# Sharing out the splitting of weights by direct and mirrored pairs, and an MLP that begins four steps later

## The chip, the cores and the metric

One core of a Trainium2 chip. The metric is device time in microseconds of the slowest (here the only) core.

## The reference

Four sequences of 3008 tokens. First an attention without softmax, then an MLP over all 12032 tokens:

```python
scores = (1.0 / S) * z @ z.T            # z: 4 x 3008 x 64
attn   = np.maximum(scores, 0.0) ** 2   # symmetric
x      = u * (attn @ v)                 # u, v: 4 x 3008 x 256
h      = x @ w_in                       # 256 -> 2048, w_in is float64
g      = h * np.clip(h + 3.0, 0.0, 6.0) / 6.0
y      = g @ w_out                      # 2048 -> 256, w_out is float64
```

## The kernel before

**Splitting.** Each operand of a matmul is split into a high and a low part of a reduced-precision type, and a product is made of three matmuls (low times high, high times low, high times high). So every `h`, `y` and `o` tile costs three passes on TensorE (PE), and VectorE (DVE) has to make every low part (`al`, `gl`, `xl`, `vl`, `w_in_l`, `w_out_l`).

**Steps.** The attention of a sequence is cut into 6 *chunks* of 512 columns (`c`), and a chunk into 12 *pairs* of 2 x 128 rows (`p`). There are 24 chunks and 288 steps, numbered through as `g`; step 12 begins chunk 1, step 24 chunk 2, step 36 chunk 3. In step g, `attend` multiplies pair g by `v` (12 matmuls into the two PSUM banks `o0` and `o1`), while `scores` works ahead on a later pair: two ahead as long as `g < FIRST`, one ahead from then on (`lead`). After the last pair of a chunk, `times_u` (L388, two DVE instructions) reads both banks, and only then can the first matmul of the next chunk write into them.

**Two kinds of pair.** A *direct* pair (`p // 2 >= c`) is computed: 4 matmuls `s`, then on ScalarE (ACT) three instructions `rt` (Relu, L320), `ah` (Square, rounded, L329) and `r` or `r2` (Square, L330), then on DVE one `al` (L340). A *mirrored* pair (`p // 2 < c`) is the transposed copy of one already computed in this sequence: no `s` matmuls, but a turn on DVE (L271), a cast on ACT (L285) and `al` on DVE (L287). Chunk 0 has no mirrored pair, chunk 1 the pairs 0 and 1, chunk 2 the pairs 0 to 3, chunk 3 the pairs 0 to 5.

**Weights.** `w_in` and `w_out` come in as float64, in 16 pieces, and each has to be split once: `split64` takes 6 DVE operations a piece (L101, L106, L110, L114, L119, L123), `finish64` two more (L131, L133), 8 in all, and one ACT cast (L117) that reads what L114 has written and that L131 waits for. The generator `weight_ops` hands them out one DVE operation at a time; `weight_work(n)` issues the next n. A piece is finished only after the next one has been split. The ACT cast is not issued where it arises but put in a list, which `flush_copies` empties: in `scores`, behind the pair's ACT instructions, or at the start of `finish64`, whichever comes first in the program. Pieces are fetched by the SP queue two pieces ahead.

**MLP.** 16 *units* a chunk of tokens: 8 times `up` (12 matmuls `h`, ACT L418, DVE L419, ACT L77, DVE `gl` L78) and 8 times `down` (12 matmuls `y`). Units are issued at the end of a step, so many that they are spread evenly over the steps from `FIRST` on; the last 20 units come after the last step. The line that says how many are to be done after step g:

```python
target = max(0, g + 1 - FIRST) * ((len(chunks) - 1) * NU - 4) // total   # total = 288 - FIRST, NU = 16
```

The order of instructions on each engine is the order of the program (`manual_schedule`); nothing is reordered later. In one step it is: `scores` of a later pair, the turn of the pair after it, `weight_work`, `attend` and `times_u`, MLP units.

Of the kernel before, what the change touches and what calls it, by code (L numbers as in the profile page):

```python
# [19 lines left out]
NPAIR = NJ // 2  # L20
# [1 line left out]
NF = DFF // P  # L22
NFP = NF // 2

FIRST = 28

TINY = 1.125 * 2.0 ** -15

# [2 lines left out]
def relu2_attention_then_hswish_mlp(  # L31
# [153 lines left out]
    def split_v(b, p):  # L185
        vh, raw = vt[b, p], raws.pop(("v", p))
        vl = vpool.tile([P, 2, D], F32R, tag="vl", name="vl")
        split(vh, vl, raw, rounded=b == 0)
        vt[b, p] = (vh, vl)

    def fetch_z(b, k):
        if b == 0:
            raw = xpool.tile([P, CH], F32, tag=("xh0", "xh1", "xl0", "xl1")[k % 4], name="zraw")
        else:
            raw = stg.tile([P, CH], F32, tag="stg", name="zraw")
        zx = zpool.tile([P, CH], F32R, tag="zx", name="zx")
        zy = zpool.tile([P, CH], F32R, tag="zy", name="zy")
        zt[b, k] = (zx, zy)
        raws["z", k] = raw
        cols = slice(k * CH, (k + 1) * CH)  # L200
        nc.sync.dma_start(out=raw, in_=zz[b, :, cols])
        if b == 0 and k > 1:
            nc.gpsimd.dma_start(out=zx[0:64], in_=zz[b, 0:64, cols])
            nc.gpsimd.dma_start(out=zy[64:128], in_=zz[b, 64:128, cols])

    def split_z(b, k):
        zx, zy = zt[b, k]
        raw = raws.pop(("z", k))
        split(zx[0:64], zy[0:64], raw[0:64], b == 0 and k > 1)
        split(zy[64:128], zx[64:128], raw[64:128], b == 0 and k > 1)  # L210
# [13 lines left out]
    def fetch_mirrored():  # L224

        while to_fetch and len(mirrored) < 2:
            b, c, p = to_fetch[0]
            if (b, p // 2, c) not in whole:
                return
            fetch_pair(*to_fetch.pop(0))  # L230

    def fetch_pair(b, c, p):


        src = kept[b, p // 2, c]
        nk = width(c) // 32
        t = lpool.tile([P, 16, 64], F32, tag="l", name="l")
        for q in range(4):
            c0 = q * P + (p % 2) * 64
            nc.sync.dma_start(  # L240
                out=t[32 * q:32 * q + 32, :nk, :],
                in_=src[:, c0:c0 + 64].rearrange("(k e) f -> e k f", e=32),
            )
        mirrored[b, c, p] = t
# [19 lines left out]
    def turn(b, c, p):  # L264

        if p // 2 >= c:
            return
        n = width(c)
        t = mirrored.pop((b, c, p))
        rn = rpool.tile([P, 2, CH], F32, tag="r", name="rm")[:, :, :n]  # L270
        nc.vector.transpose(  # L271
            out=rn.rearrange("p r (k e) -> p r k e", e=32),
            in_=t[:, :n // 32].rearrange("p k (r e) -> p r k e", r=2),
        )
        turned[b, c, p] = rn
        fetch_mirrored()

    def from_mirror(b, c, p):
        n = width(c)
        rn = turned.pop((b, c, p))  # L280
        ah = apool.tile([P, 2, CH], F32R, tag="ah", name="ah")
        al = apool.tile([P, 2, CH], F32R, tag="al", name="al")
        if urgent:
            flush()
        nc.scalar.copy(out=ah[:, :, :n], in_=rn)  # L285
        flush_copies()
        nc.vector.tensor_tensor(  # L287
            out=al[:, :, :n], in0=rn, in1=f(ah[:, :, :n]), op=ALU.subtract
        )
        at[b, c, p] = (ah, al)  # L290
        flush()
# [62 lines left out]
    def width(c):  # L354
        return CH if c < NCH - 1 else S - CH * (NCH - 1)
# [20 lines left out]
    def load_u(b, c):  # L376
        n = width(c)
        t0 = b * S + c * CH
        t = upool.tile([P, 2, CH], F32, tag="u", name="u")
        nc.sync.dma_start(  # L380
            out=t[:, :, :n], in_=ut[:, t0:t0 + n].rearrange("(k p) t -> p k t", p=P)
        )
        raw_x[b, c] = t
# [8 lines left out]
    def split_x(b, c):  # L392
        n = width(c)
        raw = raw_x.pop((b, c))
        for d in range(2):
            xh = xpool.tile([P, CH], F32R, tag=f"xh{d}", name=f"xh{d}")
            xl = xpool.tile([P, CH], F32R, tag=f"xl{d}", name=f"xl{d}")
            split(xh[:, :n], xl[:, :n], raw[:, d, :n])
            xt[d] = (xh, xl)
# [54 lines left out]
    pairs = [(b, c, p) for b, c in chunks for p in range(NPAIR)]  # L454
# [62 lines left out]
    def weight_work(n):  # L517
        for _ in range(n):
            next(w_ops, None)
# [17 lines left out]
    def maybe_split():  # L537

        if to_split and to_split[0] < avs[0]:
            i = to_split.pop(0)  # L540
            split_x(*chunks[i])
            if i + 2 < len(chunks):
                load_u(*chunks[i + 2])

    def attend(b, c, p):
        for d in range(2):
            av(b, c, p, d)
            if p == NPAIR - 1:
                times_u(b, c, d)
# [3 lines left out]
    def turn_next():  # L553

        while g_turned[0] < min(g_done + 1, len(pairs)):
            turn(*pairs[g_turned[0]])
            g_turned[0] += 1

    with tc.manual_schedule():
        nc.vector.memset(three, 3.0)  # L560
        fetch_z(0, 0)
        fetch_v(0, 0)
        split_z(0, 0)
        fetch_z(0, 1)
        fetch_v(0, 1)
        weight_work(1)
        split_v(0, 0)
        split_z(0, 1)
        scores(0, 0, 0)
        fetch_z(0, 2)  # L570
        fetch_v(0, 2)
        scores(0, 0, 1)
        fetch_v(0, 3)
        g_done = 2
        to_fetch += [(b, c, p) for b, c, p in pairs if p // 2 < c]
        g_turned = [2]
        for i, (b, c) in enumerate(chunks):
            ahead = b + 1 if c == NCH - 1 and b + 1 < B else None
            for p in range(NPAIR):
                g = i * NPAIR + p  # L580
                lead = 2 if g < FIRST else 1
                if i == 0:
                    if p + 1 < NPAIR:
                        split_v(0, p + 1)
                    if p % 2 == 0 and p // 2 + 2 < NCH:
                        split_z(0, p // 2 + 2)
                early = lead == 2 and p == NPAIR - 1
                if early:
                    attend(b, c, p)
                while g_done < min(g + lead + 1, len(pairs)):  # L590
                    scores(*pairs[g_done], square_on_act=i < 3)
                    g_done += 1
                if p > 3:
                    fetch_mirrored()
                if p < NPAIR - 1 or early:
                    turn_next()
                if i == 0:
                    if p + 4 < NPAIR:
                        fetch_v(0, p + 4)
                    if p % 2 == 0 and p // 2 + 3 < NCH:  # L600
                        fetch_z(0, p // 2 + 3)
                    if p == 6:
                        load_u(*chunks[0])
                        load_u(*chunks[1])
                maybe_split()
                if g >= FIRST:
                    weight_work(5)
                elif p < NPAIR - 2:
                    weight_work(4 if i else 2)
                if ahead and p < NPAIR - 1:  # L610
                    if p:
                        split_v(ahead, p - 1)
                    if p < NPAIR - 2:
                        fetch_v(ahead, p)
                    if p % 2 == 1:
                        fetch_z(ahead, p // 2)
                    elif p:
                        split_z(ahead, p // 2 - 1)
                elif b and c == 0 and p < 4:
                    if p in (1, 2):  # L620
                        split_v(b, NPAIR - 3 + p)
                    if p < 2:
                        fetch_v(b, NPAIR - 2 + p)
                    if p == 2:
                        fetch_z(b, NCH - 1)
                    if p == 3:
                        split_z(b, NCH - 1)
                if not early:
                    attend(b, c, p)
                    turn_next()  # L630
                if p == NPAIR - 1:
                    avs[0] += 1
                total = len(pairs) - FIRST
                target = max(0, g + 1 - FIRST) * ((len(chunks) - 1) * NU - 4) // total
                mlp_units(target - units_done[0])
        mlp_units(1)
        maybe_split()
        mlp_units(len(chunks) * NU - units_done[0])
# [35 lines left out]
```

## Time and profile before

| | |
|---|---|
| time, median of 3 runs (lowest, highest) | 1997.01 us (1996.62, 1998.65) |
| the profiled execution's own time | 1998.23 us |
| its span | 1996.4 us |
| mean granted TensorE clock | 0.994 |
| PE busy | 1959.4 us (98%) |
| DVE busy | 1280.7 us (64%) |
| ACT busy | 987.5 us (49%) |

The span runs from the first to the last instruction of the profiled execution. Busy time of an engine is the sum of its instructions; a group's idle time is what its engine stood still just before it, and the releaser named is what ended that. The chain of waits is followed back from the last instruction, at each step to what released it. Times in the timeline are microseconds from the start of the span.

### The profile page before, as it was taken

The page shows a single profiled execution, that of the slowest core. Times are in us where ns is not written, and L with a number is a line of the kernel's source. Part 1 is how long each engine was busy: PE and PEld are TensorE (multiplying, and loading weights), DVE is VectorE, ACT ScalarE, POOL GpSimd, SP SyncE. Part 2 cuts the span into 40 slices and gives each one's busy share as a digit, 9 for nine tenths or more (in the row PEclk, how much of TensorE's full clock was granted, in tenths as well). Part 3 has the DMA queues.
Part 4 walks back from the last instruction along what each step waited for, and adds up shares of the span by engine and source line. Part 5 has one row for each costly group of instructions (what it writes and reads, how often), then busy time and mean ns, then how long its engine had stood idle before and what let it go on. Part 6 is the DMA issues. An engine that isn't in the chain of part 4 may idle for free.

```text
span 1996.4 us, 22062 instructions
## 1 busy us (share of the span) xinstructions
PE 1959.4 (98%) x8688; PEld 1637.0 (82%) x8688; DVE 1280.7 (64%) x1277; ACT 987.5 (49%) x1057; POOL 14.2 (1%) x26
## 2 busy tenths in 40 slices
PE   7899999999999999999999999999999999999999
PEld 5677788788888888888888888888888888888888
DVE  5798765676556566577565665657756565666654
ACT  6665444455444444456544454444554544444343
POOL 2000000000000000000000000000000000000000
PEclk9899999999999999999999999999999999999999
DMA  9663233424323233253333232324342323332300
GB/s 266 201 160 103 64 82 72 115 71 116 82 64 81 72 74 95 50 128 89 95 82 90 55 93 53 101 62 109 90 116 61 86 59 92 74 82 60 94 10 20
DMA packets 403271, 178.14 MB, mean 89 GB/s; under 512 B 250080, under 2 KB 385248, under 8 KB 403168
## 3 DMA queue, kind: packets, MB, share of 16 engines
q1 hardware_dynamic: 399232, 172.55, 34.3%
q0 software_dynamic: 3936, 4.20, 0.9%
q8 instruction: 68, 1.11, 0.2%
q14 instruction: 35, 0.29, 0.1%
HBM read 104.07 MB, written 72.61 MB: 89 GB/s over the span
## 4 chain that ended last, share of the span: by engine, by line
PE 90%; DVE 4%; DMA 2%; ACT 2%; issue 1%; SPq 1%; DVEq 0%; ACTq 0%
PE o L73 34%; PE h L73 24%; PE y L73 24%; PE s L73 7%; DMA zraw<-in_zz_dram 1%; DVE rm L271 1%; DMA vraw<-in_v_dram 1%; DVE rt L419 1%; DVE al L287 1%; ACT rt L418 0%; ACT gh L77 0%; ACT rt L320 0%; SPq L240 0%; DVE gl L78 0%; DMA d<-r 0%
## 5 line engine op out<-in xcount | busy, mean ns | idle before, releaser
L419 DVE SCALAR_TENSOR_TENSOR rt<-rt,h 128x1024 f32<-128x1024 f32 (+1 forms) x192 | 230.0, 1198 | 420.6 <-ACT rt L418 420.4
L418 ACT ACTIVATE rt<-h,three 128x1024 f32<-128x1024 f32 (+1 forms) x192 | 211.0, 1099 | 550.2 <-PE h L73 544.4
L73 PE MATMUL o<-ah,vl 128*128 128x512 f32 (+1 forms) x1152 | 448.1, 389 | 13.3 <-DVE u L388 6.2
L73 PE MATMUL o<-ah,vh 128*128 128x512 f32 (+1 forms) x1152 | 446.8, 388 | 0.0
L73 PE MATMUL o<-al,vh 128*128 128x512 f32 (+1 forms) x1104 | 429.2, 389 | 3.5 <-DVE al L287 3.5
L73 PE MATMUL y<-gh,w_out_l 128*128 128x512 f32 (+1 forms) x768 | 296.3, 386 | 1.7 <-DVE w_out_l L133 1.7
L73 PE MATMUL y<-gl,w_out_h 128*128 128x512 f32 (+1 forms) x768 | 296.3, 386 | 1.1 <-DVE gl L78 1.1
L73 PE MATMUL y<-gh,w_out_h 128*128 128x512 f32 (+1 forms) x768 | 296.0, 385 | 0.0
L73 PE MATMUL h<-xh,w_in_l 128*128 128x512 f32 (+1 forms) x768 | 295.9, 385 | 0.0
L73 PE MATMUL h<-xl,w_in_h 128*128 128x512 f32 (+1 forms) x768 | 295.9, 385 | 0.0
L73 PE MATMUL h<-xh,w_in_h 128*128 128x512 f32 (+1 forms) x768 | 295.8, 385 | 0.0
L78 DVE TENSOR_TENSOR gl<-rt,gh 128x1024 fp32r<-128x1024 f32 (+1 forms) x192 | 230.7, 1202 | 80.5 <-ACT gh L77 77.9
L73 PEld LDWEIGHTS o<-ah,vl 128*128 128x128 f32 x1152 | 218.2, 189 | 60.6 <-issue 11.9
L77 ACT CAST gh<-rt 128x1024 fp32r<-128x1024 f32 (+1 forms) x192 | 197.2, 1027 | 122.8 <-DVE rt L419 122.8
L73 PEld LDWEIGHTS o<-ah,vh 128*128 128x128 f32 x1152 | 218.3, 189 | 40.9
L73 PEld LDWEIGHTS o<-al,vh 128*128 128x128 f32 x1104 | 209.0, 189 | 45.8 <-DVE al L287 5.7
L320 ACT ACTIVATE rt<-s 128x1024 f32<-128x1024 f32 x168 | 171.3, 1020 | 129.9 <-PE s L73 125.1
L332 DVE TENSOR_TENSOR r<-rt 128x1024 f32<-128x1024 f32 (+1 forms) x140 | 170.0, 1214 | 95.7 <-ACT rt L320 95.6
L340 DVE TENSOR_TENSOR al<-r,ah 128x1024 fp32r<-128x1024 f32 x140 | 171.0, 1221 | 22.3 <-ACT r L330 8.6
L73 PEld LDWEIGHTS y<-gh,w_out_l 128*128 128x128 f32 x768 | 144.2, 188 | 29.8 <-DVE w_out_l L133 1.3
L73 PEld LDWEIGHTS y<-gl,w_out_h 128*128 128x128 f32 x768 | 144.2, 188 | 28.9 <-DVE gl L78 2.1
L73 PEld LDWEIGHTS y<-gh,w_out_h 128*128 128x128 f32 x768 | 144.2, 188 | 27.1
(51 smaller groups left out, 1807.0 us busy)
## 6 DMA issues: line engine op xcount, KB each, us to landing
d<-r SPq DMA_DIRECT2D x220, 256.0 KB, 2.9
l<-d SPq DMA_DIRECT2D x320, 128.0 KB, 3.3
l<-d SPq DMA_DIRECT2D x160, 112.0 KB, 2.9
vraw<-in_v_dram SPq DMA_DIRECT2D x44, 256.0 KB, 3.3
u<-in_ut_dram SPq DMA_DIRECT2D x20, 512.0 KB, 4.2
out_dram<-y SPq DMA_DIRECT2D x40, 256.0 KB, 3.1
zraw<-in_zz_dram SPq DMA_DIRECT2D x24, 256.0 KB, 3.6
wraw<-in_w_in_dram SPq DMA_DIRECT2D x8, 512.0 KB, 4.5
```

The costliest lines, as they stand in the source:

```text
L73: nc.tensor.matmul(out, lhsT=lhsT, rhs=rhs, start=start, stop=stop)
L77: nc.scalar.copy(out=hi, in_=raw)
L78: nc.vector.tensor_tensor(out=lo, in0=raw, in1=f(hi), op=ALU.subtract)
L271: nc.vector.transpose(out=rn.rearrange("p r (k e) -> p r k e", e=32), in_=t[:, :n // 32].rearrange("p k (r e) -> p r k e", r=2),)
L287: nc.vector.tensor_tensor(out=al[:, :, :n], in0=rn, in1=f(ah[:, :, :n]), op=ALU.subtract)
L320: nc.scalar.activation(out=rn, in_=s[:, :, :n], func=AF.Relu, scale=1.0 / S)
L332: nc.vector.tensor_tensor(out=r2_of, in0=r_of, in1=r_of, op=ALU.mult)
L340: nc.vector.tensor_tensor(out=l_of, in0=r2_of, in1=h_of, op=ALU.subtract)
L418: nc.scalar.activation(out=rn, in_=h, func=AF.Relu, bias=three)
L419: nc.vector.scalar_tensor_tensor(out=rn, in0=rn, scalar=6.0, in1=h, op0=ALU.min, op1=ALU.mult)
```

## The change

Three things are changed. `FIRST` goes from 28 to 32, so that MLP units begin with step 32 (and `lead` becomes 1 there). In the steps of chunks 1 and 2 before `FIRST`, the number of weight operations no longer is 4 in the pairs 0 to 9 and 0 in the pairs 10 and 11, but depends on the kind of the pair scored last (two ahead of the step): 5 where it is direct, 1 where it is mirrored. From `FIRST` on it is 5 where the pair scored last is direct and 4 where it is mirrored, in place of 5 always. The steps of chunk 0 stay as they are.

```diff
-FIRST = 28
+FIRST = 32
...
+    def is_mirrored(b, c, p):
+        return p // 2 < c
...
                 maybe_split()
+                direct = not is_mirrored(*pairs[g_done - 1])
                 if g >= FIRST:
-                    weight_work(5)
-                elif p < NPAIR - 2:
-                    weight_work(4 if i else 2)
+                    weight_work(5 if direct else 4)
+                elif i == 0:
+                    weight_work(2 if p < NPAIR - 2 else 0)
+                else:
+                    weight_work(5 if direct else 1)
```

Weight operations by step: before, 40 in the steps 12 to 21, none in 22 and 23, 16 in 24 to 27, 5 a step from 28 on. Now 50 in the steps 12 to 21, 4 in 22 to 25, 30 in 26 to 31, 15 in 32 to 34, 4 in 35 and in 36, and the rest in 37. In front of the step 36 the MLP has done 11 units before, 5 now.

How this moves instructions, at three places. The numbers behind the names tell tiles apart; line numbers of the changed kernel are 3 higher from L276 on.

**First place: ACT, between the pairs 15 and 16** (chunk 1). `rt_...`, `ah_...`, `r2_...` are the three instructions of a direct pair, `w_in_h<-t0_646` is the cast of a weight piece. Before:

```order
L320 ACTIVATE rt_696<-s_691 128x1024
L329 ACTIVATE ah_697<-rt_696 128x1024
L330 ACTIVATE r2_700<-rt_696 128x8x4x32
L117 CAST w_in_h_91<-t0_646 128x2x256
L320 ACTIVATE rt_732<-s_727 128x1024
```

Now:

```order
L117 CAST w_in_h_91<-t0_646 128x2x256
L323 ACTIVATE rt_701<-s_696 128x1024
L332 ACTIVATE ah_702<-rt_701 128x1024
L333 ACTIVATE r2_705<-rt_701 128x8x4x32
L323 ACTIVATE rt_735<-s_730 128x1024
```

The cast has moved from behind the three instructions of pair 16 to ahead of them, since the step now issues L114 and the next piece's L131 together. The same happens at pair 19 and at pair 32; at the pairs 17, 20 and 22 the cast stays behind.

**Second place: DVE, from the last pair of chunk 1 to its `times_u`** (L388, L391 now). Before:

```order
L344 TENSOR_TENSOR al_935<-r2_937,ah_934 128x512
L347 TENSOR_TENSOR ah_934<-r2_937,ah_934 64x512
L271 STREAM_TRANSPOSE rm_944<-l_560 128x1024
L110 TENSOR_SCALAR wraw_842<-wraw_842 128x512
L114 SCALAR_TENSOR_TENSOR t0_913<-wraw_842,t0_913 128x512
L119 TENSOR_SCALAR wraw_842<-t0_913 128x512
L123 SCALAR_TENSOR_TENSOR w_in_l_92<-wraw_842 128x2x256
L287 TENSOR_TENSOR al_968<-rm_944,ah_967 128x1024
L271 STREAM_TRANSPOSE rm_972<-l_587 128x1024
L388 TENSOR_TENSOR u_449<-u_449,o0_649 128x512
L388 TENSOR_TENSOR u_449<-u_449,o1_656 128x512
```

Now:

```order
L350 TENSOR_TENSOR ah_947<-r2_950,ah_947 64x512
L271 STREAM_TRANSPOSE rm_957<-l_560 128x1024
L114 SCALAR_TENSOR_TENSOR t0_925<-wraw_854,t0_925 128x512
L119 TENSOR_SCALAR wraw_854<-t0_925 128x512
L123 SCALAR_TENSOR_TENSOR w_out_l_94<-wraw_854 128x512
L131 TENSOR_TENSOR t0_858<-t0_858,w_in_h_91 128x512
L133 TENSOR_TENSOR w_in_l_92<-t0_858,w_in_l_92 128x2x256
L290 TENSOR_TENSOR al_985<-rm_957,ah_984 128x1024
L271 STREAM_TRANSPOSE rm_988<-l_587 128x1024
L101 TENSOR_SCALAR t0_995<-wraw_921 128x512
L391 TENSOR_TENSOR u_449<-u_449,o0_650 128x512
L391 TENSOR_TENSOR u_449<-u_449,o1_657 128x512
```

Between the pair's `al` and `times_u` stand six weight operations now, four before; from the start of chunk 1 to `times_u` it is 51, and it was 40.

**Third place: DVE, up to the `times_u` of chunk 2.** `al_1517` and `al_1449` are of pair 36, L419 and L78 (L422 and L78 now) belong to the MLP. Before:

```order
L133 TENSOR_TENSOR w_out_l_94<-t0_1312,w_out_l_94 128x512
L101 TENSOR_SCALAR t0_1490<-wraw_1358 128x512
L287 TENSOR_TENSOR al_1517<-rm_1477,ah_1516 128x1024
L106 SCALAR_TENSOR_TENSOR t0_1490<-wraw_1358,t0_1490 128x512
L110 TENSOR_SCALAR wraw_1358<-wraw_1358 128x512
L114 SCALAR_TENSOR_TENSOR t0_1490<-wraw_1358,t0_1490 128x512
L119 TENSOR_SCALAR wraw_1358<-t0_1490 128x512
L123 SCALAR_TENSOR_TENSOR w_out_l_94<-wraw_1358 128x512
L388 TENSOR_TENSOR u_640<-u_640,o0_1032 128x512
```

Now:

```order
L422 SCALAR_TENSOR_TENSOR rt_1443<-rt_1443,h_1430 128x1024
L290 TENSOR_TENSOR al_1449<-rm_1391,ah_1448 128x1024
L78 TENSOR_TENSOR gl_1445<-rt_1443,gh_1444 128x1024
L106 SCALAR_TENSOR_TENSOR t0_1402<-wraw_1284,t0_1402 128x512
L110 TENSOR_SCALAR wraw_1284<-wraw_1284 128x512
L114 SCALAR_TENSOR_TENSOR t0_1402<-wraw_1284,t0_1402 128x512
L119 TENSOR_SCALAR wraw_1284<-t0_1402 128x512
L391 TENSOR_TENSOR u_640<-u_640,o0_1045 128x512
```

Four weight operations stand between pair 36's `al` and `times_u` now, five before; a `gl` of the MLP has come in between.

## Rows read from the trace of the kernel before

**Rows 1.** Section 1 of the page: busy time of each engine, its share of the span and its instructions.

```profile
PE 1959.4 (98%) x8688; PEld 1637.0 (82%) x8688; DVE 1280.7 (64%) x1277; ACT 987.5 (49%) x1057; POOL 14.2 (1%) x26
```

**Rows 2.** Busy time of each engine in four stretches: us of the stretch, busy us of PE, PEld, DVE, ACT, POOL with their instructions, granted TensorE clock, share of the DMA engines, GB/s.

```profile
78.00:120.00 42.00, 38.57 (x171) 31.59 (x169) 39.24 (x57) 33.90 (x38) 0.00 (x0) 1.00 0.66 185
120.00:137.40 17.40, 17.13 (x69) 14.02 (x70) 15.99 (x22) 9.51 (x10) 0.00 (x0) 0.90 0.74 181
...
185.00:222.00 37.00, 32.45 (x137) 25.11 (x136) 33.77 (x43) 14.24 (x16) 0.00 (x0) 1.00 0.44 97
222.00:360.00 138.00, 138.00 (x610) 114.08 (x610) 83.33 (x75) 62.59 (x63) 0.00 (x0) 1.00 0.29 70
```

**Rows 3.** What PE waited for from 78 to 232 us: engine and tile waiting <- engine, tile and line waited for: us in total, times, longest.

```profile
PE o L73 <- DVE u L388: 5.2, 2, 3.7
PE y L73 <- DVE w_out_l L133: 1.7, 2, 0.9
PE o L73 <- DVE al L287: 1.3, 2, 0.9
```

**Rows 4.** The chain of waits in order of time, four pieces: start us, us, what (xcount of matmuls).

```profile
71.14 3.38 PE o L73 x10
...
82.57 0.91 PE s L73 x4
83.48 2.72 PE o L73 x12
...
120.27 7.32 PE o L73 x24
```

**Rows 5.** DVE in order of time over two steps of chunk 1: start us, us, line, operation, out<-in. L340 is a pair's `al` (of the pairs 15, 16 and 17), the other lines are operations of the weight splitting.

```profile
84.25 1.22 DVE L340 TENSOR_TENSOR al<-rt,ah 128x1024 fp32r<-128x1024 f32 x1
85.38 0.42 DVE L110 TENSOR_SCALAR wraw<-wraw 128x512 uint32<-128x512 uint32 x1
85.84 0.69 DVE L114 SCALAR_TENSOR_TENSOR t<-wraw,t 128x512 f32<-128x512 f32 x1
86.57 0.43 DVE L119 TENSOR_SCALAR wraw<-t 128x512 uint32<-128x512 uint32 x1
87.03 0.69 DVE L123 SCALAR_TENSOR_TENSOR w_in_l<-wraw 128x512 fp32r<-128x512 uint32 x1
87.64 1.22 DVE L340 TENSOR_TENSOR al<-r,ah 128x1024 fp32r<-128x1024 f32 x1
88.77 0.68 DVE L131 TENSOR_TENSOR t<-t,w_out_h 128x512 f32<-128x512 f32 x1
89.49 0.69 DVE L133 TENSOR_TENSOR w_out_l<-t,w_out_l 128x512 fp32r<-128x512 f32 x1
90.10 0.42 DVE L101 TENSOR_SCALAR t<-wraw 128x512 uint32<-128x512 uint32 x1
...
91.17 1.22 DVE L340 TENSOR_TENSOR al<-r,ah 128x1024 fp32r<-128x1024 f32 x1
```

**Rows 6.** ACT in order of time, the same columns, with the idle time before an instruction and what ended it in brackets.

```profile
86.56 0.62 ACT L117 CAST w_in_h<-t 128x512 fp32r<-128x512 f32 x1
87.20 1.03 ACT L320 ACTIVATE rt<-s 128x1024 f32<-128x1024 f32 x1
...
89.23 1.05 ACT L330 ACTIVATE r<-rt 128x1024 f32<-128x1024 f32 x1
...
147.42 0.62 ACT L117 CAST w_out_h<-t 128x512 fp32r<-128x512 f32 x1 [2.08 <-DVE t L114]
147.94 1.11 ACT L418 ACTIVATE rt<-h,three 128x1024 f32<-128x1024 f32 x1
```

**Rows 7.** DVE in order of time, at the ends of chunks 1 and 2. L388 x2 is `times_u`, L271 the turn of a mirrored pair, L344 the first half of the `al` of a chunk's last pair.

```profile
112.34 0.69 DVE L344 TENSOR_TENSOR al<-r,ah 128x512 fp32r<-128x512 f32 x1 [0.33 <-ACT r L330]
...
118.31 1.24 DVE L271 STREAM_TRANSPOSE rm<-l 128x1024 f32<-128x1024 f32 x1
119.47 1.25 DVE L388 TENSOR_TENSOR u<-u,o 128x512 f32<-128x512 f32 x2
...
124.26 1.23 DVE L287 TENSOR_TENSOR al<-rm,ah 128x1024 fp32r<-128x1024 f32 x1 [1.17 <-ACT ah L285]
...
192.17 1.28 DVE L388 TENSOR_TENSOR u<-u,o 128x512 f32<-128x512 f32 x2
```

**Rows 8.** PE in order of time: the first matmul behind each of three waits, with the idle time before it and what ended it.

```profile
71.14 0.47 PE L73 MATMUL o<-ah,vl 128*128 128x512 f32 x1 [2.21 <-DVE vl L78]
...
120.27 0.69 PE L73 MATMUL o<-ah,vl 128*128 128x512 f32 x1 [3.70 <-DVE u L388]
...
192.99 0.47 PE L73 MATMUL o<-ah,vl 128*128 128x512 f32 x1 [1.49 <-DVE u L388]
```

**Rows 9.** What PE waited for from 232 us to the end.

```profile
PE o L73 <- DVE al L287: 2.2, 4, 1.0
PE o L73 <- ACT ah L285: 1.4, 1, 1.4
PE y L73 <- DVE gl L78: 1.1, 2, 0.8
PE o L73 <- DVE u L388: 1.0, 2, 0.5
```

**Rows 10.** DMA issues, section 6 of the page: out<-in, queue, xcount, KB each, median us from issue to landing.

```profile
wraw<-in_w_in_dram SPq DMA_DIRECT2D x8, 512.0 KB, 4.5
```

## The prediction

> **What bounds the kernel now.** I began with the busy times: PE is busy for 98% of the span, DVE for 64% [rows 1]. Over the whole, PE sets the time, and the change leaves PE's work as it is: it can only change how long PE waits or runs slow. So I asked next where PE waits. From 78 to 232 us, the stretch that the change touches, it waits for DVE alone, 8.2 us in all, the two longest for `times_u` at the ends of chunks 1 and 2, 3.70 and 1.49 us [rows 3, 8]. The stretches say why: from 78 to 120 us (steps 13 to 23) DVE is busy 39.24 of 42.0 us, 93%, and from 185 to 222 us 91%; from 222 to 360 us, when the weights are done, 60%, and there PE never waits [rows 2]. So beside the splitting of the weights DVE is nearly full, and the question is what five operations a step in place of four do to a queue that is 93% full.
>
> **One step of chunk 1.** PE needs 0.91 us for `s` and 2.72 us for `o`, 3.63 us a direct step [rows 4]. DVE, counted from start to start, needs 1.13 us for `al` (84.25 to 85.38); from 84.25 to 91.17 us stand two `al` and eight weight operations, 6.92 us, so an operation costs (6.92 - 2.26) / 8 = 0.58 us [rows 5]. With four that is 1.13 + 2.33 = 3.46 us, and DVE gains 0.17 us a step on PE. With five it is 4.04 us, and DVE loses 0.41 us a step, for ten steps. DVE's start is small: the `al` of pair 15 ends at 85.47 us, and `o` of step 15 begins at 83.48 + 3.63 = 87.11 us [rows 4, 5], 1.6 us later. By step 18 or so it is used up, and from then on PE waits for `al`.
>
> **First sum: up to the first `times_u`** (at 119.47 us before [rows 7]). DVE works in order, and ahead of `times_u` stand 51 weight operations where 40 stood: 11 x 0.58 = 6.4 us. On top come waits of DVE that the trace of before does not have. Where L114 and the next piece's L131 fall into one step, the cast is issued ahead of the next pair's `rt`, and ACT cannot begin that pair before DVE has done L114. From the start of a cast to the end of `r`, ACT takes 86.56 to 90.28 us, 3.7 us [rows 6]; behind L114, DVE has only L119, L123, L131 and L133 to do, 0.46 + 0.61 + 0.72 + 0.61 = 2.4 us [rows 5]. So DVE stands 1.3 us in front of the `al` of pair 16, and 1.9 us at pair 19, where L133 comes later. That ACT is really held so, rows show: a cast waited 2.08 us for L114, and the activation behind it began 0.52 us after it [rows 6]. Less an idle 0.33 us of DVE in the old stretch [rows 7], the sum is 6.4 + 3.2 - 0.3 = **+9.3 us**: `times_u` at 128.8 us, PE back 0.8 us later, as before [rows 7, 8]. That PE waits a part of this in small pieces at the pairs 16 to 23 and the rest, 5 to 6 us, at step 24 changes nothing in the sum.
>
> **Second sum: from there to the second `times_u`** (at 192.17 us [rows 7]). From the end of the first, at 130.0 us, DVE has 52 weight operations (30.2 us), twelve `al` (1.13 each, 1.44 where it is cut in two: 13.9), three turns (118.31 to 119.47, 1.16 each [rows 7]: 3.5) and three `up` units with two instructions of the size of `al` each (6.8): 54.4 us. It stands idle where its input is late: 1.1 us for the cast of pair 26, as once before (1.17 [rows 7]). 2.2 us at pair 28: PE begins step 24 at 129.6 us, takes 7.3 us for the steps 24 and 25, as before [rows 4], and 0.9 for `s`, ACT 3.1 (87.20 to 90.28 [rows 6]), so 140.9 us, and DVE is through at 138.7. 1.3 us at pair 32 for the cast, as above. 1.8 us at pair 34, whose `rt` stands behind a cast and the first L418: 0.6 + 1.1 + 3.1 us on ACT behind L114, 2.9 on DVE. That makes 130.0 + 54.4 + 6.4 = 190.8 us, and PE begins step 36 at 191.7. Before, it began there at 192.99 us [rows 8], but had done 11 units by then, not 5; a unit has 12 matmuls, as `o` of a step, 2.72 us [rows 4], so what compares is 192.99 - 16.3 = 176.7 us. The delay at step 36 is **+15.0 us**, with a wait of over 4 us for `times_u` in it.
>
> **The clock.** After the wait of 3.70 us PE took 7.32 us for 24 matmuls that else take 5.44, 1.9 us lost, and that stretch was granted 0.90: part of it ran at the lower level of 1.2 GHz. After 1.49 us nothing of the kind shows: granted 1.00 [rows 2, 4, 8]. Behind the wait of step 24 this loss is there in both versions. Behind step 36 the wait is new in size: **+1.9 us**, between 0 and 1.9.
>
> The Trainium skill has a rule that speaks against the change: by "TensorE: Matmul & The Clock Gate", section "A second HAM failure mode: psum-queue depth-cycling", short and frequent idle times between groups of matmuls can make PE's clock go down and up again and again. The row nearest to that does not bear it out: from 185 to 222 us PE stood still for 4.5 us in short waits, at a granted clock of 1.00 [rows 2, 3]. I take nothing for it in the sum; what it would give is the second rival.
>
> **What goes.** The waits between 199 and 222 us, 1.7 us for `w_out_l` and 1.3 us for `al` [rows 3]: where eleven units were done by step 36, it is five, so the pieces are ready long before, and DVE has less to do there. **-3.0 us**, between -3.0 and 0.
>
> **What costs nothing.** Fetches of weights go past others on SP, but stay two pieces, over three steps and so more than 10 us, ahead, and land in 4.5 us [rows 10]; the u tile of chunk 3, of the same size, is loaded at step 42 rather than 38, five steps before it is used. Without this cover each would cost its landing. POOL's queue is not moved. That units lie 1.42 a step rather than 1.40 costs nothing where PE is never idle. The waits after 232 us, 5.7 us in all [rows 9], fall on other units now: between -3 and +3, I take 0.
>
> **Sum.** 15.0 + 1.9 - 3.0 = +13.9 us. The profiled execution took 1998.2 us, 1.2 above the median of the runs, so it would take 2012.1; for the median, 1997.0 + 13.9 = **2011 us**, 0.7% slower.
>
> **Rivals.** About 0.2% (4 us) is what a measurement of this kernel can tell from no change.
> 1. *Faster: the direct steps hide the fifth operation, and the later MLP frees the stretch after 185 us.* PE's waits for the second `times_u`, `w_out_l` and `al` go, 1.5 + 3.0 us: 1992.5 us. It decides at (3.63 - 1.13) / 5 = 0.50 us an operation. For it: before, PE never waits for the `al` of a direct pair (L340) [rows 3]. Against it: the rows say 0.58, with DVE without a gap in them [rows 5]. 5%.
> 2. *The short waits lower the clock.* Waits of 0.2 to 2 us at the pairs 16 to 23, 32 and 34 slow PE down, as 2.21 us did at 71.14 us: 10 matmuls took 3.38 us behind it, where 2.27 is the rule [rows 4, 8]. Against it, the granted 1.00 above. Four stretches of 1.9 us: 2011 + 7.6 = 2018.6 us. 12%.
> 3. *ACT is not held by the casts, or catches up elsewhere,* so that only DVE's added work counts: 15.0 - 3.2 - 6.4 + 1.9 - 3.0 = +4.3, 2001.3 us, or 1999.4 without the loss of clock. Against it: ACT works in order [rows 6]. 9%, mostly within 0.2%.
> 4. *The change does not bite*, because pieces are drawn ahead when the MLP needs them, and so stand where they stood. Against it: the order has 51 operations ahead of `times_u`. 1997 us, 2%.
>
> **How the numbers follow.** The forecast has the 72% left. Its bounds: a loss of clock at step 36 of 0 or 1.9, later waits of -3 to +3, and 9.6 us of DVE's waits, which rest on an order of arrival and may come out a third smaller: 2003 to 2014. With rival 2 above and the upper half of rival 3 below, the range is 2002 to 2018. Slower by over 0.2%: 72 + 12 and 2 of rival 3, 86%. Within: 7 of rival 3 and 2 of rival 4, 9%. Faster: 5%.
>
> **What would show it.** In the changed profile: DVE without idle time from 85 to 190 us but for waits for ACT; `times_u` of chunk 1 near 129 us with a wait of PE of 5 to 6 us, that of chunk 2 near 191 us with over 4; DVE idle 1 to 2 us in front of the `al` of the pairs 16, 19 and 32, ended by ACT `r`; PE waiting for `al` at the pairs 18 to 23; no wait for `w_out_l`; a granted clock below 1 twice. I am wrong if `times_u` of chunk 1 starts before 124 us, or if PE makes up more than 3 us after step 36.

## The result and the profile after

The changed kernel takes **2026.24 us** (median of 4 runs, 2025.21 to 2027.41), the kernel before on the same chip 1996.82: a ratio of 1.0143 (95% interval 1.0131 to 1.0156), 29 us slower. The direction was right, the size was not: 2011 was forecast, 2018 was the top of the range. The profiled execution took 2025.7 us, 27.5 more than that of before.

All times below are of profiled executions unless they are called medians. Behind L276 the line numbers of the changed kernel are higher by 3: `al` of a direct pair is L343, of a mirrored one L290, `times_u` L391, the MLP's two elementwise operations L421 and L422.

The stretches first, as in [rows 2], and with one more from 360 us (us of the stretch, busy us of PE, PEld, DVE, ACT, POOL, granted clock, DMA share, GB/s):

```profile
78.00:120.00 42.00, 39.01 (x158) 29.97 (x157) 37.55 (x58) 31.20 (x35) 0.00 (x0) 0.96 0.61 182
120.00:137.40 17.40, 11.63 (x42) 8.88 (x42) 15.79 (x20) 5.55 (x6) 0.00 (x0) 0.80 0.68 148
185.00:222.00 37.00, 32.81 (x133) 26.55 (x132) 25.79 (x29) 12.49 (x13) 0.00 (x0) 0.91 0.35 72
222.00:360.00 138.00, 137.58 (x607) 113.49 (x605) 84.75 (x78) 63.37 (x66) 0.00 (x0) 1.00 0.28 69
360.00:425.00 65.00, 59.37 (x255) 49.97 (x256) 42.76 (x46) 31.79 (x41) 0.00 (x0) 0.95 0.46 118
```

PE did 42 matmuls in the second where it had done 69, at 0.80; the third was granted 0.91 where it had 1.00. From 222 to 360 us it is nearly as before. The last shows what the forecast did not have: in the same 65 us the kernel before has PE busy for 61.91 us with 282 matmuls, this one for 59.37 us with 255.

What PE waited for, first from 78 to 232 us (against [rows 3]):

```profile
PE o L73 <- DVE u L391: 10.0, 2, 5.8
PE o L73 <- DVE al L343: 3.4, 4, 1.7
PE h L73 <- ACT rt L323: 1.5, 1, 1.5
PE o L73 <- DVE al L347: 0.4, 1, 0.4
```

and from 232 us to the end (against [rows 9]):

```profile
PE o L73 <- DVE al L290: 5.0, 7, 1.1
PE y L73 <- ACT gh L77: 4.0, 1, 4.0
PE o L73 <- DVE u L391: 3.8, 6, 1.3
PE y L73 <- DVE gl L78: 1.5, 2, 0.8
PE o L73 <- ACT ah L288: 1.3, 1, 1.3
PE h L73 <- ACT rt L323: 1.2, 1, 1.2
```

15.3 us in the first where 8.2 stood, 16.8 us in the second where 5.7 stood. These are waits without what the clock loses behind them. DVE in order of time (idle time before, and what ended it, in brackets), the `al` of the pairs 16 and 19, the first `times_u`, the `al` of pair 28 (against [rows 7]):

```profile
89.17 1.23 DVE L343 TENSOR_TENSOR al<-r,ah 128x1024 fp32r<-128x1024 f32 x1 [1.14 <-ACT r L333]
...
103.08 1.22 DVE L343 TENSOR_TENSOR al<-r,ah 128x1024 fp32r<-128x1024 f32 x1 [1.86 <-ACT r L333]
...
127.34 1.27 DVE L391 TENSOR_TENSOR u<-u,o 128x512 f32<-128x512 f32 x2
...
139.80 1.23 DVE L343 TENSOR_TENSOR al<-rt,ah 128x1024 fp32r<-128x1024 f32 x1 [2.33 <-ACT rt L333]
```

And PE: the first matmul behind four waits, at pair 19, at the steps 24 and 36 (against [rows 8]) and at the first change of sequence:

```profile
104.36 0.76 PE L73 MATMUL o<-al,vh 128*128 128x512 f32 x1 [1.70 <-DVE al L343]
...
128.16 0.77 PE L73 MATMUL o<-ah,vl 128*128 128x512 f32 x1 [5.77 <-DVE u L391]
...
190.40 0.77 PE L73 MATMUL o<-ah,vl 128*128 128x512 f32 x1 [4.19 <-DVE u L391]
...
400.79 0.49 PE L73 MATMUL y<-gh,w_out_l 128*128 128x512 f32 x1 [4.01 <-ACT gh L77]
```

The first three are of the kind that was forecast. The fourth is not in the forecast.

**A ledger of lost time.** To place the whole, I counted at each group of matmuls the time so far less what the matmuls up to there take at full clock (2.72 us for twelve of 512 columns [rows 4], in proportion to columns). The total work is 1930.5 us in every kernel, so the growth of the difference over the same work is time lost, to waits or to the clock. Up to 76 us it is 30 to 32 us in all the kernels below, differing from run to run, so I count from there. Each row of the table is one profiled execution. The stretches: up to step 26 of PE's work (about 127 us before), up to 300 us of work (345 us), the three changes of sequence (work 300 to 400, 780 to 900, 1300 to 1420 us), and what lies between and after. In us:

| kernel | to step 26 | to work 300 | change 1 | change 2 | change 3 | the rest |
|---|---|---|---|---|---|---|
| before | 5.6 | 6.4 | 5.4 | 1.2 | 2.8 | 8.5 |
| changed | 14.6 | 10.5 | 11.1 | 7.3 | 3.9 | 11.2 |
| new sharing, start at 28 | 14.5 | 2.4 | 5.8 | 1.2 | 1.9 | 8.5 |
| old sharing, start at 32 | 6.4 | 8.2 | 9.2 | 6.8 | 4.2 | 11.5 |
| old sharing, start at 31 | 5.4 | 5.1 | 3.7 | 5.0 | 7.2 | 6.8 |
| new sharing, start at 31 | 14.6 | 3.3 | 1.9 | 4.7 | 5.9 | 6.8 |
| changed, fetches on POOL | 14.7 | 8.9 | 1.6 | 1.6 | 2.0 | 11.2 |
| before, fetches on POOL | 6.9 | 6.6 | 2.0 | 1.2 | 0.8 | 8.5 |

Early, in the first two columns, the change loses 25.1 - 12.0 = **13.1 us** more than before: 13.9 was forecast. Late, in the other four, it loses 33.5 - 17.9 = **15.6 us** more: "between -3 and +3, I take 0" was forecast. Of these 15.6 us, 12.9 are lost at the three changes of sequence and 2.7 elsewhere; 11.1 are longer waits (16.8 less 5.7), the rest is lost behind them. So the large error is in one term, and most of the study is on where it comes from.

**What happens near 400 us.** In the last chunk of a sequence v and z of the next are fetched and split. ACT in the changed kernel, step 64:

```profile
394.53 0.62 ACT L77 CAST vh<-vraw 128x512 fp32r<-128x512 f32 x1 [6.37 <-DMA vraw<-in_v_dram]
396.00 0.62 ACT L77 CAST zx<-zraw 64x512 fp32r<-64x512 f32 x1 [0.85 <-DMA zraw<-in_zz_dram]
396.65 0.61 ACT L77 CAST zy<-zraw 64x512 fp32r<-64x512 f32 x1
397.29 1.11 ACT L421 ACTIVATE rt<-h,three 128x1024 f32<-128x1024 f32 x1
399.69 1.04 ACT L77 CAST gh<-rt 128x1024 fp32r<-128x1024 f32 x1 [1.29 <-DVE rt L422]
```

ACT stands 6.37 us for a load, and behind this cast in its queue is the `rt` of an `up` unit whose `h` PE had finished near 391.6 us. It is unit 45, the last `up` of a chunk. What follows on PE is `o` of step 65 and that step's two units, 46 and 47, both `down`, with nothing in between; the second needs this `gh`, hence the 4.01 us. The load is late in SP's queue (start us, us, issue), which experiment 3 tests:

```profile
387.14 1.87 SPq L240 DMA_DIRECT2D l<-d  x4
389.11 0.43 SPq L177 DMA_DIRECT2D vraw<-in_v_dram  x1
389.64 0.41 SPq L201 DMA_DIRECT2D zraw<-in_zz_dram  x1
```

The fetch stands behind four `l<-d` transfers, which wait for a turn on DVE to free their buffer. In what SP waited for from 360 to 425 us (us in total, times, longest) this comes first:

```profile
SPq L240 <- DVE rm L271: 31.4, 7, 9.7
```

Once issued, this load took 5.4 us (389.11 to 394.53), more than the median of 3.6 us of all loads of `vraw`, so the queue is not the whole of the delay.

The kernel before has the same hold, even a longer one, and ACT's waits for `vraw` after 232 us are 39.4 us in all there and 42.1 here. But there another unit stands behind the cast. ACT in the kernel before, step 62:

```profile
383.90 0.62 ACT L77 CAST vh<-vraw 128x512 fp32r<-128x512 f32 x1 [7.13 <-DMA vraw<-in_v_dram]
...
387.29 1.12 ACT L418 ACTIVATE rt<-h,three 128x1024 f32<-128x1024 f32 x1
...
389.69 1.04 ACT L77 CAST gh<-rt 128x1024 fp32r<-128x1024 f32 x1 [0.46 <-DVE rt L419]
```

This is unit 48, the first of a chunk, and before its `gh` is used PE has an `o`, another `up` and another `o` to do. PE waited 2.4 us, for `ah` and `al` of a pair. So the theory: **(P)** where the MLP's units stand against the steps decides which of them is held behind a late load, and the later beginning moved them. The rivals: **(B)** the late loss is the weights' backlog, paid late; **(S)** the later the MLP begins, the more is lost, whatever the step.

### The profile page after: what moved, and what is told of

It reads as the page before. It is cut to its first block, busy times and chain, and to the rows that moved or that the text cites. A ratio compares the mean times of both kernels' runs of the same rounds, so it can differ in the third digit from the quotient of the medians.

```text
span 2023.9 us, 22070 instructions
## 1 busy us (share of the span) xinstructions
PE 1969.9 (97%) x8688; PEld 1641.9 (81%) x8688; DVE 1280.6 (63%) x1277; ACT 986.9 (49%) x1057; POOL 14.2 (1%) x26
## 4 chain that ended last, share of the span: by engine, by line
PE 84%; DVE 7%; ACT 3%; DMA 3%; issue 2%; SPq 1%; DVEq 0%; ACTq 0%
PE o L73 31%; PE h L73 23%; PE y L73 23%; PE s L73 7%; DMA zraw<-in_zz_dram 2%; DVE rt L422 1%; ACT rt L421 1%; DVE al L343 1%; DMA vraw<-in_v_dram 1%; DVE al L290 1%; DVE gl L78 1%; DVE rm L271 1%; ACT gh L77 1%; ACT rt L323 0%; SPq L240 0%
## 5 line engine op out<-in xcount | busy, mean ns | idle before, releaser
L422 DVE SCALAR_TENSOR_TENSOR rt<-rt,h 128x1024 f32<-128x1024 f32 (+1 forms) x192 | 230.0, 1198 | 445.0 <-ACT rt L421 444.8
L421 ACT ACTIVATE rt<-h,three 128x1024 f32<-128x1024 f32 (+1 forms) x192 | 210.9, 1098 | 562.2 <-PE h L73 541.2
L73 PE MATMUL o<-ah,vl 128*128 128x512 f32 (+1 forms) x1152 | 450.9, 391 | 20.5 <-DVE u L391 13.8
L78 DVE TENSOR_TENSOR gl<-rt,gh 128x1024 fp32r<-128x1024 f32 (+1 forms) x192 | 230.6, 1201 | 76.6 <-ACT gh L77 74.2
L343 DVE TENSOR_TENSOR al<-r,ah 128x1024 fp32r<-128x1024 f32 x140 | 170.9, 1221 | 24.6 <-ACT r L333 11.0
L73 PEld LDWEIGHTS y<-gh,w_out_l 128*128 128x128 f32 x768 | 144.6, 188 | 31.7 <-ACT gh L77 4.9
L73 PEld LDWEIGHTS h<-xh,w_in_l 128*128 128x128 f32 x768 | 144.4, 188 | 30.6 <-ACT rt L323 3.5
L73 PEld LDWEIGHTS y<-gl,w_out_h 128*128 128x128 f32 x768 | 144.7, 188 | 29.5 <-DVE gl L78 2.7
```

Source lines behind the costliest of these rows:

```text
L73: nc.tensor.matmul(out, lhsT=lhsT, rhs=rhs, start=start, stop=stop)
L78: nc.vector.tensor_tensor(out=lo, in0=raw, in1=f(hi), op=ALU.subtract)
L343: nc.vector.tensor_tensor(out=l_of, in0=r2_of, in1=h_of, op=ALU.subtract)
L421: nc.scalar.activation(out=rn, in_=h, func=AF.Relu, bias=three)
L422: nc.vector.scalar_tensor_tensor(out=rn, in0=rn, scalar=6.0, in1=h, op0=ALU.min, op1=ALU.mult)
```

## The experiments

**1. The new sharing alone** (the changed kernel, with the old beginning):

```
-FIRST = 32
+FIRST = 28
```

> The changed kernel with the MLP beginning at step 28 again, the new sharing of the weights kept. Theory A (two causes: the sharing costs early, up to about 230 us; the later beginning of the MLP costs late, at the changes of sequence near 400 and 890 us, because other units of the MLP fall there): the 51 weight operations ahead of the first times_u stay, so PE waits 5 to 6 us at step 24 and +9 us are lost by then; in chunk 2 about 2 us of it come back, since four operations are left in place of five in the mirrored steps; late, nothing is lost beyond the kernel before. 1997 + 7 = 2004 us (2001 to 2009). Theory B (the weights are the cause of the late loss too, the backlog is only paid late): 2017 to 2024 us, with the waits after 360 us as in the changed kernel.

2002.07 us (before 1998.53; ratio 1.0020, 1.0011 to 1.0030), theory A. PE's waits from 78 to 232 us begin with

```profile
PE o L73 <- DVE u L391: 6.5, 2, 5.8
```

The wait of 5.8 at step 24 is there, and the loss up to step 26 is that of the changed kernel, 14.5 us. Of the 8.9 us that this is above before, 4.0 come back in chunk 2 (2.4 us where before loses 6.4; about 2 were expected), and late nothing is lost beyond before: 17.4 against 17.9 us. Theory B falls: the sharing costs nothing late.

**2. The later beginning alone** (the kernel before, with)

```
-FIRST = 28
+FIRST = 32
```

> The kernel before with the MLP beginning at step 32, the old sharing (four operations a step, five from the beginning of the MLP) kept. Theory A: no loss early, PE waits about 3.7 us at step 24 as before, the waits for w_out_l go (-2 us); late the changes of sequence 1 and 2 lose 6 us each beyond the kernel before: 1997 - 2 + 12 = 2007 us (2003 to 2012). Theory B: without the new sharing nothing is lost late: 1993 to 1997 us.

2015.24 us (ratio 1.0087, 1.0072 to 1.0102), above the range of theory A. Late it loses 31.7 us, 13.8 more than before, in the same waits as the changed kernel. From 232 us:

```profile
PE o L73 <- DVE al L287: 5.1, 7, 1.1
PE o L73 <- DVE u L388: 3.8, 6, 1.3
PE y L73 <- ACT gh L77: 3.4, 1, 3.4
```

Some 10 us were expected and 17 came. Late I had counted the first two changes only (12 us, where 13.8 came in all). And I had expected 2 us less in chunk 2 without the waits for `w_out_l`; they went, but the wait for the second `times_u` grew (the two waits for `u` are 8.7 us in all, 5.2 before [rows 3]): DVE had the same weights to do, and PE five units to do beside it in place of eleven.

**3. The fetches on another queue** (the changed kernel, for the sequences 1 to 3):

```
-        for dst, queue in ((raw, nc.sync), (vh, nc.gpsimd))[:1 if b else 2]:
+        for dst, queue in ((raw, nc.gpsimd if b else nc.sync), (vh, nc.gpsimd))[:1 if b else 2]:
...
-        nc.sync.dma_start(out=raw, in_=zz[b, :, cols])
+        (nc.gpsimd if b else nc.sync).dma_start(out=raw, in_=zz[b, :, cols])
```

> The changed kernel with the fetches of v and z for the sequences 1 to 3 on POOL's DMA queue, where nothing else waits, in place of SP's, where they stand behind the l<-d transfers, which wait for turns on DVE. Theory A1 (at a change of sequence ACT stands for vraw, because its fetch is issued late on SP, and the MLP's rt, gh and y stand behind that cast): the waits of ACT for vraw shrink from 6 us to under 2, and of the 20 us lost at the three changes of sequence 8 to 15 go: 2014 us (2011 to 2018). Theory A2 (the fetch is late by its staging buffer or by the transfer itself, the queue does not matter): 2023 to 2026 us with ACT's waits for vraw as they were. If a POOL fetch begins or lands later than one of SP: slower than 2026.

2008.04 us (ratio 1.0051, 1.0036 to 1.0066): 18 us below the changed kernel, more than A1 gave. ACT does not wait for `vraw` at all after 232 us (42.1 us before the edit). The cast, and the `rt` and `gh` of the same unit 45:

```profile
386.58 0.61 ACT L77 CAST vh<-vraw 128x512 fp32r<-128x512 f32 x1
...
390.21 1.12 ACT L421 ACTIVATE rt<-h,three 128x1024 f32<-128x1024 f32 x1 [1.85 <-PE h L73]
392.62 1.05 ACT L77 CAST gh<-rt 128x1024 fp32r<-128x1024 f32 x1 [1.29 <-DVE rt L422]
```

ACT now stands ready and waits for `h`. PE's waits after 232 us, all of them:

```profile
PE o L73 <- DVE u L391: 3.8, 6, 1.3
PE o L73 <- DVE al L290: 1.6, 4, 0.5
```

SP still waits for the turns, 29.5 us from 360 to 425 us (31.4 without the edit), so it is not that the turns came earlier. The three changes of sequence lose 5.2 us together, where they lost 22.3. The fetch for the cast at 386.58 us was issued on POOL's queue at

```profile
378.60 0.72 POOL L177 DMA_DIRECT2D vraw<-in_v_dram  x1 [6.25 <-DVE vl L78]
```

11.6 us before PE had finished the `h` of unit 45; on SP's it was 2.5 us (389.11 and 391.6 us). So it is shown that the loss at the changes of sequence comes about by the place of the fetches in SP's queue: 17.1 us of it go with the move.

In the list of DMA issues (KB each, median us from issue to landing) `vraw` on POOL's queue has

```profile
vraw<-in_v_dram POOLq DMA_DIRECT2D x33, 256.0 KB, 3.6
```

and in the changed kernel, on SP's,

```profile
vraw<-in_v_dram SPq DMA_DIRECT2D x44, 256.0 KB, 3.6
```

By these medians a transfer is no faster on one than on the other; what differs is when it is issued. The Trainium skill, "DMA: Bandwidth & Descriptors", section "Issuing engines are not separate DMA queues", says that issuing from several engines only saves the sequencer's time to start a transfer, which is usually small. By that the move would be worth little; it was worth 18 us here, because a transfer that is free to go no longer stands behind one that waits.

**4. The same move in the kernel before** (the two lines of experiment 3, nothing else).

> The kernel before with the same move of the v and z fetches to POOL's queue. Theory A1: of the 8 us lost there at the three changes of sequence (3.9, 1.3 and 2.8 us) half or more goes: 1991 us (1989 to 1994). Theory A2: 1996 to 1998 us.

1992.53 us (ratio 0.9974, 0.9963 to 0.9984), as A1 gave: the changes lose 4.0 us in place of 9.4. So the hold cost something before, too, but only 5 us; the change made 17 of it.

**5. One step earlier, old sharing** (the kernel before, with):

```
-FIRST = 28
+FIRST = 31
```

> The kernel before with the MLP beginning at step 31. With 32 the last up unit of a chunk (unit 45) is issued in step 64, an even one, whose queue on ACT holds the casts of v and z that wait for their load; with 31 it is issued in step 63, an odd one, with a cast of v alone. Theory P (the place of the MLP's units decides): no wait of PE for gh near 400 us, the loss at the first change of sequence is about 4 us as in the kernel before, not 8: 2009 us (2005 to 2012). Theory S (the loss grows steadily with the step at which the MLP begins): a wait for gh of 2 to 3 us is there near 400 us, and three quarters of the 16.7 us that 32 cost: 2011 us (2010 to 2014). The wait near 400 us tells them apart, the time hardly.

1998.33 us (ratio 1.0010, 1.0001 to 1.0020). P had the place right and the time too high; S had neither. There is no wait for `gh` near 400 us, change 1 loses 3.7 us, and the whole is not 17 us slower than before, as with 32, but 1. A loss that goes from 17 to 1 us with one step of 288 is no matter of "later". The late loads themselves have not gone: ACT still waits 37.6 us for `vraw` after 232 us (39.4 before, 43.3 with 32). One thing does not come for nothing: at change 3 it loses 7.2 us, more than any other kernel here, and PE waits 1.4 us for `gh` there and 1.3 at change 2. Which change is hit moves with the beginning.

**6. One step earlier, new sharing** (the changed kernel, with):

```
-FIRST = 32
+FIRST = 31
```

> The changed kernel, new sharing kept, with the MLP beginning one step earlier, at step 31. Theory P (the late loss hangs on the step in which the last up unit of a chunk is issued at a change of sequence): unit 45 falls in step 63, there is no wait of 4 us for gh near 400 us, and of the 32 us lost after 232 us about 12 go; the early loss stays within 2 us: 2012 us (2009 to 2016), which is what the prediction had for the whole change. Theory S (the later the MLP begins, the more is lost late, whatever the step): 2020 to 2024 us.

2005.12 us (ratio 1.0046, 1.0029 to 1.0063), below the range of theory P and 21 us below the changed kernel by one step. Late it loses 19.3 us, 14.2 less. ACT in step 63:

```profile
379.13 0.62 ACT L77 CAST vh<-vraw 128x512 fp32r<-128x512 f32 x1
380.47 1.12 ACT L421 ACTIVATE rt<-h,three 128x1024 f32<-128x1024 f32 x1 [0.72 <-PE h L73]
383.40 1.05 ACT L77 CAST gh<-rt 128x1024 fp32r<-128x1024 f32 x1 [1.81 <-DVE rt L422]
```

Unit 45 now stands behind a cast whose load is there. Late loads still come in the steps 64 and 65, but behind them is not the end of a chunk. The holds have moved as well, though: ACT stands 0.99 us for `vraw` in step 64, where it was 6.37, and 4.39 in step 65 (37.8 us in all after 232 us, 42.1 in the changed kernel). So one step of shift changes both which unit stands behind a hold and how long the hold is there, and no run here takes the two apart. The other 7 us are early, which I had not expected: chunk 2 loses 3.3 us where the changed kernel loses 10.5. With 31, seven units are done by step 36 in place of five (36 - 31 or 36 - 32 steps of 1.42). They are 5.4 us more for PE, and since only one of them is an `up`, 2.3 more for DVE. So DVE is 3 us less late at the second `times_u`. PE's waits for `times_u` from 78 to 232 us say so, 0.9 us at step 36 in place of 4.2:

```profile
PE o L73 <- DVE u L391: 6.7, 2, 5.8
```

And behind the shorter wait the clock stays up: from 190 to 198 us it was granted 1.00, where the changed kernel had 0.59 and lost 3.0 us.

**7. Early: the casts held ACT** (the changed kernel; `finish64` issues only the cast that it needs itself):

```
-        flush_copies()
+        flush_copies(f0)
```

where `flush_copies(f0)` issues nothing if the cast of `f0` has been issued, and otherwise the casts up to it.

> The changed kernel, but the finishing of a piece issues only its own cast: four casts (at the pairs 16, 19, 32 and 34) move behind that pair's r on ACT. Theory A (DVE stands in front of those pairs' al because ACT holds them behind a cast that waits for L114): DVE's idle times of 1.1 and 1.9 us there go, the first times_u comes 3 us earlier, PE at step 36 is 5 to 6 us earlier: 2020 us (2018 to 2023). Theory B (DVE's operations alone set the time, what is not waited for at one place is at the next): 2025 to 2027 us.

2021.09 us (before 1997.56; ratio 1.0117, 1.0102 to 1.0132), theory A. The idle times in front of the pairs 16 and 19 are gone; DVE reaches the first `times_u` at

```profile
125.40 1.27 DVE L391 TENSOR_TENSOR u<-u,o 128x512 f32<-128x512 f32 x2
```

1.9 us earlier, or 3.1 counted from 76 us, up to which this run had lost 1.2 us more. The wait of PE for `al` of direct pairs falls from 3.4 to 1.1 us. Early it loses 17.9 us in place of 25.1, some 7 where 6 were worked out.

**8. Early: the number of operations** (on top of the last one, four operations in the direct steps of chunk 1):

```
-                    weight_work(5 if direct else 1)
+                    weight_work((5 if i > 1 else 4) if direct else 1)
```

> As the kernel with only its own cast, and in chunk 1 the direct steps do four weight operations in place of five: ten operations fewer stand ahead of the first times_u. Theory A (each operation ahead of times_u costs its 0.58 us on PE's path): the first times_u another 5.8 us earlier, PE waits about 3 us or less at step 24, and the second times_u comes earlier by about as much, so 6 us below the kernel with only its own cast: 2014 us (2011 to 2017). Theory C (a fifth operation hides beside a direct step, so its number does not matter): no more than 1 us below it.

2016.28 us (ratio 1.0099, 1.0082 to 1.0116), 5 us below the last one and near theory A. PE goes on behind the two `times_u` at

```profile
121.78 0.77 PE L73 MATMUL o<-ah,vl 128*128 128x512 f32 x1 [4.92 <-DVE u L391]
...
181.95 0.77 PE L73 MATMUL o<-ah,vl 128*128 128x512 f32 x1 [4.63 <-DVE u L391]
```

4.4 and 4.0 us earlier than with five. DVE also stood 0.93 us for ACT once where it had not, so ten operations were worth 4.4 + 0.9 = 5.3 us, about 0.53 each, where 0.58 was taken. That PE would wait 3 us or less at step 24 was wrong: it waits 4.92, since it comes there earlier as well.

**9. Better versions.** The kernel before with both edits, POOL's queue and each piece's own cast:

> The kernel before with the v and z fetches on POOL's queue and each piece issuing only its own cast. Four casts move here too, at pairs that lie after 130 us, where PE waits 1.3 us for al and 1.5 us for the second times_u. Theory A: 1 to 2 us below the kernel with POOL's queue alone: 1991 us (1989 to 1993). Theory B: the same as that kernel, 1992 to 1994 us.

1992.90 us (ratio 0.9978, 0.9969 to 0.9987): the same as with POOL's queue alone, theory B. And old sharing, a beginning at step 31, and POOL's queue:

> The old sharing, the MLP beginning at step 31, the v and z fetches of the later sequences on POOL's queue. Theory P with A1 (the place of the units matters only because ACT stands for late loads): ACT does not wait for vraw, of the 20 us lost after 232 us with step 31 on SP's queue 7 go: 1991 us (1988 to 1994), the same as step 28 with POOL's queue within 3 us. Theory S2 (place and queue cost apart from each other): 1995 to 1998 us.

**1988.47 us** (before 1997.17; ratio 0.9956, 0.9940 to 0.9973), the lowest median of all (the interval of its ratio overlaps that of experiment 4), 9 us faster than before and some 38 faster than the changed kernel. What PE waits for after 250 us is one row:

```profile
PE o L73 <- DVE al L287: 0.9, 3, 0.3
```

The 7.2 us of change 3 that the beginning at 31 cost on SP's queue are 0.8 here. With no late load in ACT's queue the place of the units hardly matters: the changes of sequence lose 4.0 us with 28 and 5.2 with 32, and 2.4 with 31 in place of 15.9.

## Why the prediction was wrong, by its steps

- **The first sum held.** DVE reached the first `times_u` at 127.3 us; 128.8 was forecast, and this run was about 1 us ahead at 76 us. The two holds were forecast at 1.3 and 1.9 us and are 1.14 and 1.86, the wait at step 24 at 5 to 6 and is 5.77, the hold at pair 28 at 2.2 and is 2.33, those at the pairs 32 and 34 at 1.3 and 1.8 and are 1.14 and 1.73. Experiments 7 and 8 show both terms by themselves.
- **The second sum held.** PE began step 36 at 190.4 us (forecast 191.7), the wait there was 4.19 (over 4). By the ledger PE is at that place 14.7 us behind before (forecast 15.0). That units which are begun later are cover that DVE loses was in the sum; experiment 6 shows how strong it is, 7 us for two units, with the clock.
- **The clock** lost 3.0 us behind step 36; 1.9 was forecast, and as the most. There is one more loss, of 1.7 us, behind the wait of 1.70 at 104.36 us; the second rival had this at 12%, for four places. It came at one of the small waits, and not at the others (0.53, 0.98 and 1.47 us at 90, 159 and 169 us). It cost nothing by step 24: DVE has no idle time from 104 us to the first `times_u`, so PE only waited less for it. Of the rule that the forecast named beside it, the Trainium skill's "TensorE: Matmul & The Clock Gate", section "A second HAM failure mode: psum-queue depth-cycling", this trace shows one case: the clock went down behind a short wait and up again. That it does so again and again, no run here shows.
- **What goes** went, and more: there is no wait for `w_out_l`, and the 4.7 us that the ledger of the kernel before grows by behind the wait at step 36, up to 232 us, are not there; 3.0 was forecast. So the early sum is 14.7 + 3.0 - 4.7 = 13.0 us by the ledger. That it comes as near 13.9 as it does is in part luck: the last two terms are off by 1.1 and 1.7 us in opposite directions.
- **The failed step is the last of those that "cost nothing": "the waits after 232 us, 5.7 us in all, fall on other units now: between -3 and +3, I take 0".** The lost time after 300 us of work, which it stood for, measures +15.6 us, of which 11.1 are waits; 12.9 are lost at the changes of sequence, where ACT's holds for late loads became PE's waits. I sized the term by what PE waited for before [rows 9], and took the sum of these waits as a bound on how far they could move. It is none. ACT stood 39 us for `vraw` in the kernel before, in holds of up to 7.1 us, and PE showed 3.6 us of waits for that at the most (those for `ah` and `al`), because other work lay between. When the cover moves, a hold of 6.4 us can become a wait of 4.0 and a slow stretch behind it. The rows that I went by say what PE waited for, and none says what ACT waited for at that place.
- For the range this means that the term should have reached from about -5 (the whole of what the holds cost before, experiment 4) to +15; the forecast of the likeliest would still have been hard to place, since steps 31 and 32 lie 21 us apart.

What stays open: at change 2 the loss (7.3 us) lies in five pieces near 880 to 920 us, mostly at `al` and `ah` of mirrored pairs, and goes with the late loads too (1.6 in experiment 3), but I did not take a single unit there and move it. The kernels of the experiments 7 and 8, which begin at 32 as well, lose 10.7 and 7.4 us there, and 8.7 and 8.3 at change 1, so single places differ by some us among kernels with the same beginning.

The six short waits for `times_u` after 232 us, 3.8 us in place of 1.0, are there in all kernels that begin at 32, on either queue, and in none that begins at 31 (1.0 us, two waits, with 28). The order of PE's work in the traces says where: each stands where a single MLP unit lies between the last `o` of a chunk and the first of the next, and the unit ahead of that last `o` is an `up`, whose last two DVE instructions (L422 and `gl`) stand ahead of `times_u` (before the first of them, at 360.09 us, from 355.78 to 359.35 us). That holds for all six in the changed kernel and for both before. With a beginning at 31 two units lie at every change of chunk. So these waits, too, seem to hang on where the units fall, and not on the late loads; no run moved a unit there to show it.

## What to carry to other kernels

An edit that shifts one stream of work against another, by so little as one step in 288, has to be held against every periodic hold of the in-order queues it passes, not only against the waits of the engine that sets the time: list what the off-path engines wait for, with the longest single hold, and ask which instruction would stand behind it. A hold that costs little now can cost much when the phase changes. It is better taken away (here by giving the loads a queue on which nothing else waits, two lines) than worked around by the choice of a start; and work that is begun later is cover lost for whatever was hidden behind it.

## What the runs showed of the hardware that was not expected

What the clock loses behind a wait does not grow with the wait: behind 1.70, 5.77, 4.19 and 4.01 us of waiting it was 1.7, 1.8, 3.0 and 3.3 us (growth of the ledger from the first matmul behind the wait on, less further waits). The four stretches of the changed kernel (us of the stretch, busy us of PE, granted clock, DMA share, GB/s):

```profile
103.00:110.00 7.00, 5.64 (x18) 0.76 0.65 174
128.00:136.00 8.00, 7.84 (x27) 0.77 0.65 141
190.00:198.00 8.00, 7.60 (x21) 0.59 0.48 100
398.00:411.00 13.00, 9.45 (x29) 0.74 0.43 111
```

Behind the last the matmuls of 512 columns begin 0.43 us apart, 403.06 and 403.49 for example, where 0.23 is the rule: the lower level of 1.2 GHz. From 393.9 to 410 us the ledger grows by 8.2 us, of which 4.8 are waits (4.01 and 0.77) and 3.4 the clock and the start behind the wait.
